# V and the large convolutions in 64x128 row tiles, as two halves with swapped PSUM banks, interleaved with K and R

## The chip, the cores and the metric

The kernel runs on one core of one Trainium2 chip. The core has a matrix engine (PE, TensorE), a vector engine (DVE), an activation engine (ACT), a general engine (POOL) and a sync engine (SP), each of which works through its own instructions in order, and 16 DMA engines that they share. Matmuls read SBUF and write PSUM, which has 128 partitions and 8 banks of 512 fp32 each. The metric is the time of one execution on the device, in microseconds (us); a lower one is better.

## The reference

x is 8 sequences of 4160 rows of 192 channels. A causal convolution of 7 taps comes first, with softmaxed weights shared by the 24 channels of each of 8 heads; then a channel mix:

```python
# attention stage: y[s, h, :] = sum over k of softmax(weight)[h, k] * x[s - 6 + k, h, :]
out = np.einsum('hk,bskhg->bshg', w, x_unf)
...
# channel mix on y
x_prev = np.concatenate([np.zeros((B, 1, D), dtype=np.float32), x[:, :-1, :]], axis=1)
xk = mu_k * x + (1.0 - mu_k) * x_prev
xr = mu_r * x + (1.0 - mu_r) * x_prev
k = np.maximum(xk @ w_k, 0.0)            # 192 -> 1024
v = k * k @ w_v                          # 1024 -> 192
r = 1.0 / (1.0 + np.exp(-(xr @ w_r)))    # 192 -> 192
return (r * v).astype(np.float32)
```

## The kernel before, in words

**Pairs, steps, bundles.** The 8 sequences are worked in 4 pairs. A pair is cut into steps of 512 rows (256 at both ends of the first pair), and the last 64 rows of all sequences make a step at the end. Channels lie on partitions: yT holds 64 channels of one sequence on partitions 0 to 63 and of the other on 64 to 127, three times for 192. So K and R contract 64 rows at a time, and a matmul of the first sequence stands on the upper half of PE's array (rows 0 to 63), one of the second on the lower half, each with its own PSUM bank: 64x128 row tiles. A step of 512 rows needs 8 slots of K (128 of the 1024 hidden channels for both sequences, six matmuls of 512 columns, L520); a bundle is four slots. There are 65 bundles. R (`r`, L594) and V (`v`, L606, `v_mm`, L577) are worked in quads of 256 rows of both sequences, one of each in a bundle. V contracts 128 hidden channels at a time on the whole array: 32 matmuls of 192 columns a quad.

**Convolution.** x is loaded by POOL's DMA queue, casting to bf16, in groups of 120-row blocks (`groups`, L86). A conv matmul multiplies a banded matrix `toe` (128x128 per head) with a block of x. Groups 0 to 2 (`conv_small`) and 3 (`conv_full`, L331) use the whole array with blocks of 120 rows that share 6 rows with the block before. Groups 4 and up (`conv_mm`, L309) hold each block as two halves of 58 rows and use 64x64 tiles, four at a time; `load_x_halves` (L118) loads them so. A unit is as many heads as fill a PSUM bank; ACT evicts a unit (`conv_out`, L385). Groups 0 to 3 are transposed on PE (`tr`). The others go to DRAM (`y_write`, L393, four DMAs on SP's queue) and come back transposed (`y_read`, L403, one transposing DMA on SP's queue).

**Elementwise work.** DVE makes d = y[s] - y[s-1] (`diff`, L473), xk and xr = mu * d + y[s-1] (`mix`, L496 and L500), k squared (L563) and the product r * v from PSUM (L618). ACT applies relu to K (L549) and the sigmoid to R (L602). The product leaves by two DMAs a quad on SP's queue (L626).

**Order.** The order on every engine is written out by hand (`manual_schedule`): tables say which bundle issues what, and the loop at L764 walks the bundles: four slots of K and their relus, R, V, mixes, three squares, the product, the conv units, the last square, then `late` with y writes and reads. A group's units stand in the bundles 10 to 7 before its step's first bundle; its write stands in the bundle of the last unit, its read two bundles later (one for group 4). All PSUM tiles come from one ring of four buffers of two banks (`ring`, L53), so a tile waits until the tile four places before is read.

Of the kernel before, what the change touches and what calls it, by code (L numbers as in the profile page):

```python
# [10 lines left out]
ALU = mybir.AluOpType  # L11
# [3 lines left out]
def kernel(  # L15
# [23 lines left out]
    HB = 58  # L39
# [46 lines left out]
    groups, base = [], []  # L86
    for p in range(NPAIR):
        blk0 = 0
        for nb, s, on_pe in (
            ((3, 0, True), (4, 1, True), (4, 2, True), (5, 3, True), (10, 4, False), (10, 6, False))  # L90
            if p == 0
            else ((10, 0, False), (10, 2, False), (10, 4, False), (6, 6, False))
        ):
            groups.append((p, blk0, nb, first_bundle[first_step[p] + s], on_pe))
            if on_pe:
                base.append(blk0 * BLK)
            elif groups[-2][4] or blk0 == 0:
                base.append(blk0 * BLK)
            else:
                base.append(base[-1] + 2 * HB * groups[-2][2])  # L100
            blk0 += nb
# [4 lines left out]
    def x_tile(g):  # L106
        p, blk0, nb, _, _ = groups[g]
        xb = three.tile([P, GB, 2, D], BF16, tag="xb", name="xb")
        xbs[g] = xb
        if g > 4:  # L110

            nc.vector.memset(xb[0:1, 0, 0, 0:2], 0.0)
        if blk0 == 0:
            nc.gpsimd.memset(xb[0:32, 0, :, :], 0.0)  # L114
        if g > 3 and base[g] + 2 * HB * nb >= S:
            nc.gpsimd.memset(xb[:, nb - 1, :, :], 0.0)

    def load_x_halves(g):  # L118
        p, _, nb, _, _ = groups[g]
        xb = xbs[g]  # L120
        for s in range(2):
            b = 2 * p + s
            for i in range(2):
                full = []
                for m in range(nb):
                    r0 = base[g] + (2 * m + i) * HB - HALO
                    lo, hi = max(0, -r0), min(Q, S - r0)
                    if lo == 0 and hi == Q:
                        full.append(m)
                    elif hi > lo:  # L130
                        nc.gpsimd.dma_start(  # L131
                            out=xb[i * Q + lo : i * Q + hi, m, s, :], in_=x[b, r0 + lo : r0 + hi, :]
                        )
                nc.gpsimd.dma_start(  # L134
                    out=xb[i * Q : (i + 1) * Q, full[0] : full[-1] + 1, s, :],
                    in_=bass.AP(
                        tensor=x.tensor,
                        offset=x.offset + (b * S + base[g] + (2 * full[0] + i) * HB - HALO) * D,
                        ap=[[D, Q], [2 * HB * D, len(full)], [1, D]],
                    ),  # L140
                )

    def load_x(g):
        p, blk0, nb, _, _ = groups[g]
        if g > 3:
            return load_x_halves(g)
        xb = xbs[g]
        for s in range(2):
# [5 lines left out]
            t0 = blk0 * BLK - HALO  # L154
            nc.gpsimd.dma_start(  # L155
# [144 lines left out]
    def pieces(c0, c1):  # L300
        cuts = [c0] + [a for a in range(Q, D, Q) if c0 < a < c1] + [c1]
        return list(zip(cuts, cuts[1:]))

    def conv_units(g):
        n = min(H, BANK // (G * groups[g][2]))
        return [range(h, min(H, h + n)) for h in range(0, H, n)]


    def conv_mm(g, c):  # L309
        nb = groups[g][2]  # L310
        if c == 0:
            ys[g] = two.tile([P, GB, 2 * D], BF16, tag="y", name="y")
        ps = ring.tile([P, 2, BANK], FP32, tag="k", name="ps_c")
        hs = conv_units(g)[c]
        w = G * len(hs)
        nn = nb // 2
        conv_ps[g, c] = ps
        for k, h in enumerate(hs):
            for j in range(2):
                for i in range(2):  # L320
                    nc.tensor.matmul(  # L321
                        out=ps[j * Q : (j + 1) * Q, i, 0 : nb * w].rearrange("p (n s c) -> p n s c", n=nn, s=2)[
                            :, :, :, k * G : (k + 1) * G
                        ],
                        lhsT=toe[i * Q : (i + 1) * Q, h, i * Q : (i + 1) * Q],
                        rhs=xbs[g][i * Q : (i + 1) * Q, j * nn : (j + 1) * nn, :, h * G : (h + 1) * G],
                        start=True,
                        stop=True,
                    )

    def conv_full(g, c, copy):  # L331
        nb = groups[g][2]
        if c == 0:
            ys[g] = two.tile([P, GB, 2 * D], BF16, tag="y", name="y")
        y = ys[g][:BLK, :nb, :].rearrange("p n (c s q) -> p n c s q", c=NC, s=2)
        ps2 = ring.tile([P, 2, BANK], FP32, tag="k", name="ps_c")
        w = 2 * G
        banks = [ps2[:, k, 0 : nb * 2 * w].rearrange("p (n s c) -> p n s c", n=nb, s=2) for k in range(2)]
        for k, ps in enumerate(banks):
            for i in range(2):  # L340
                h = 4 * c + 2 * k + i
                nc.tensor.matmul(
                    out=ps[:, :, :, i * G : (i + 1) * G],
                    lhsT=toe[:, h, :],
                    rhs=xbs[g][:, :nb, :, h * G : (h + 1) * G],
                    start=True,
                    stop=True,
                )
        for k, ps in enumerate(banks):
            c0 = (4 * c + 2 * k) * G  # L350
            for a, b in pieces(c0, c0 + w):
                copy(
                    out=y[:, :, a // Q, :, a % Q : a % Q + b - a], in_=ps[:BLK, :, :, a - c0 : b - c0]
                )
# [22 lines left out]
    def conv_out(g, c, copy):  # L377
        nb = groups[g][2]
        hs = conv_units(g)[c]
        ps = conv_ps.pop((g, c))  # L380
        c0, c1 = hs[0] * G, hs[-1] * G + G
        src = ps[:, :, 0 : nb * (c1 - c0)].rearrange("p i (n s c) -> p i n s c", n=nb // 2, s=2)
        y = ys[g][:, :nb, :].rearrange("p (n i) (c s q) -> p i n c s q", i=2, c=NC, s=2)
        for a, b in pieces(c0, c1):
            copy(out=y[:, :, :, a // Q, :, a % Q : a % Q + b - a], in_=src[:, :, :, :, a - c0 : b - c0])  # L385

    def new_yT(p):
        yTs[p] = two.tile([P, 3, -(-(YC + NBLK * BLK) // 16) * 16], BF16, tag="yT", name="yT")
        y_drams[p] = dram.tile([S + 2 * P, 2 * D], BF16, tag=f"y{p % 2}", name="y_dram")
# [3 lines left out]
    def y_write(g):  # L393
# [3 lines left out]
        for j in range(2):  # L397
            r0 = base[g] + j * nb * HB
            rows = y_drams[p][r0 : r0 + nb * HB, :].rearrange("(n t) c -> t n c", t=HB)
            for t0, t1 in ((0, HB // 16 * 16), (HB // 16 * 16, HB)):  # L400
                nc.sync.dma_start(out=rows[t0:t1], in_=ys[g][j * Q + t0 : j * Q + t1, :nb, :])

    def y_read(g):  # L403
        p, blk0, nb, _, _ = groups[g]
        r0 = base[g] // 16 * 16
        r1 = min((base[g] + 2 * nb * HB) // 16 * 16, S)
# [70 lines left out]
    def mix(s, i, sl=slice(0, NC)):  # L477
# [3 lines left out]
        if sl.start == 0:  # L481
            (xks, xrs)[i][s] = two.tile([P, NC, STEP], BF16, tag=("xk", "xr")[i], name=("xk", "xr")[i])
        t = (xks, xrs)[i][s]
        if s == 0 and i == 0:
            c = sl.start
# [9 lines left out]
        for c in range(sl.start, sl.stop):  # L495
            nc.vector.tensor_scalar(  # L496
                out=t[:, c, :L], in0=d[:, c, :L], scalar1=mu[:, i, c : c + 1], scalar2=None, op0=ALU.mult
            )
        o = shaped(s, t[:, sl, :L])
# [111 lines left out]

    def tile_of(s, j, k):
# [37 lines left out]
    early, first, rq, xt, mixes, vq, vo, late = ({} for _ in range(8))  # L650
# [4 lines left out]
    def conv(g, c):  # L655
        if g < 3:
            act_, dve_ = nc.scalar.copy, nc.vector.tensor_copy
            return conv_small(g, (act_, act_, dve_ if g == 0 else act_))
        if g == 3:
            return conv_full(g, c, nc.scalar.copy)  # L660
        conv_mm(g, c)
        conv_out(g, c, nc.scalar.copy)

    for g, (p, blk0, nb, fb, on_pe) in enumerate(groups):
        nx = len(conv_units(g))
# [8 lines left out]
        for i, b in enumerate(xs):  # L674
            at(xt, b, conv, g, i)
# [13 lines left out]
    for s, (p, t0, L, n0, ns) in enumerate(steps):  # L689
# [4 lines left out]
        at(mixes, fb - 1, diff, s)  # L694
        at(mixes, fb - 1, mix, s, 0)
        at(mixes, last_bundle[s] - (s < LAST), mix, s, 1)
        if s == LAST - 1 or s < LAST and steps[s + 1][0] > p:
            at(late, fb - 1, keep_tail, p)
    for s, j, vb in quads:
        if s == LAST:  # L700
            at(late, vb, v_last, s, j)
            at(rq, vb - 1, r, s, j)
        else:
            at(vq, vb, v, s, j)
            at(vo, vb, v_out, s, j)
            at(rq, vb - 1, r, s, j)
# [51 lines left out]

    with tc.manual_schedule():
        prologue()  # L760
        for b in range(-20, 0):
            for table in (early, first, rq, xt, mixes, vq, vo, late):
                assert b not in table, b
        for b in range(quads[-1][2] + 1):  # L764
            ns = bundles[b] if b < len(bundles) else ()
            run(early, b)
            for part in (ns[:2], ns[2:]) if b == 0 else (ns,):
                if part:
                    k_section(part)
                for n in part:  # L770
                    k_relu(n)
# [44 lines left out]
```

## Time and profile before

| what | value |
|---|---|
| median of three runs | 434.31 us (433.28 to 436.19) |
| the profiled execution | 434.77 us, span 433.1 us |
| PE | 418.1 us busy, 5045 matmuls |
| DVE | 378.4 us busy, 678 instructions |
| ACT | 348.2 us busy, 427 instructions |
| POOL | 62.4 us busy, 101 instructions |
| mean granted PE clock | 0.999 |
| DMA | 64.73 MB, mean 149 GB/s |

Busy times are a share of the span, from the first instruction to the last; what the execution has beside its span (1.7 us) is start and end. An engine's busy share says how full it is, not whether its work decides the end: that is read from the chain of work that ended last, followed back from the last instruction. In a row of groups, `L577 PE MATMUL ps_v<-wv,k 128*128 128x192 bf16` is line 577, an operation of PE that writes ps_v from wv and k, on 128 x 128 of the array, with 192 columns streamed. Matmuls overlap, so a row's mean duration (246 ns for V) is longer than the distance between two starts. SPq is SP's instruction queue, whose DMA issues are not counted as busy.

### The profile page before, as it was taken

What the parts mean: (1) busy time and instruction counts of PE and PEld (TensorE: products, weight loads), DVE (VectorE), ACT (ScalarE), POOL (GpSimd) and SP (SyncE); (2) the same over time, 40 slices, a digit from 0 to 9 for tenths busy, and PEclk for the clock granted to TensorE, in tenths of its full rate; (3) what the DMA queues carried; (4) which work ended last, traced back from release to release, by engine and by line L of the source; (5) the groups of instructions that cost most, each with busy time, mean ns of one, the idle gap of its engine ahead of it and who ended that gap; (6) DMA issues with size and microseconds to landing.
All of it is one profiled execution on the core that took longest, in us unless ns stands there. A gap on an engine that the chain in (4) does not pass through costs nothing.

```text
span 433.1 us, 12070 instructions
## 1 busy us (share of the span) xinstructions
PE 418.1 (97%) x5045; PEld 293.4 (68%) x5045; DVE 378.4 (87%) x678; ACT 348.2 (80%) x427; POOL 62.4 (14%) x101
## 2 busy tenths in 40 slices
PE   7779999989999999999999999999999999999995
PEld 3456667757867766776677667766766776667785
DVE  5879888798988899888889989888898889999983
ACT  5787988978988888888889878988898888777780
POOL 7651002203310200303030200203000000000000
PEclk9999999999999999999999999999999999999999
DMA  7998885999896976689896994496845484321223
GB/s 127 192 160 126 201 175 107 183 232 184 176 184 180 175 196 124 89 197 156 195 183 160 181 208 108 97 222 126 192 116 136 118 205 87 111 66 47 74 75 109
DMA packets 136444, 64.73 MB, mean 149 GB/s; under 512 B 87122, under 2 KB 136006, under 8 KB 136390
## 3 DMA queue, kind: packets, MB, share of 16 engines
q1 hardware_dynamic: 96536, 48.29, 47.2%
q0 software_dynamic: 38960, 15.08, 30.2%
q8 instruction: 39, 0.64, 0.6%
q10 hardware_dynamic: 894, 0.61, 0.5%
q14 instruction: 15, 0.12, 0.1%
HBM read 30.75 MB, written 36.96 MB: 156 GB/s over the span
## 4 chain that ended last, share of the span: by engine, by line
PE 85%; DMA 5%; DVE 4%; ACT 3%; issue 2%; POOL 1%; SPq 0%; ACTq 0%
PE ps_v L577 39%; PE ps_k L520 35%; PE ps_r L594 7%; PE ps_c L321 3%; DMA yT<-y_dram 3%; ACT k_sb L549 2%; DMA wk<-in_moe_w_k_dram 2%; DVE k L563 1%; DVE xk L496 1%; PE ps_t L420 1%; ACT y L385 0%; DVE d L473 0%; DVE o_sb L618 0%; POOL xb L155 0%; DVE yT L429 0%
## 5 line engine op out<-in xcount | busy, mean ns | idle before, releaser
L549 ACT ACTIVATE k_sb<-ps_k 128x1024 bf16<-128x1024 f32 x260 | 246.4, 1047 | 23.3 <-PE ps_k L520 23.0
L520 PE MATMUL ps_k<-xk,wk 64*128 64x512 bf16 (+1 forms) x1632 | 181.0, 367 | 3.5 <-ACT k_sb L549 1.2
L577 PE MATMUL ps_v<-wv,k 128*128 128x192 bf16 x2080 | 182.7, 246 | 1.3 <-ACT k_sb L549 1.3
L577 PEld LDWEIGHTS <-k 128*128 128x128 bf16 x2080 | 168.7, 98 | 11.3 <-issue 11.3
L563 DVE TENSOR_TENSOR k<-k_sb 128x1024 bf16<-128x1024 bf16 x260 | 167.3, 685 | 0.4 <-ACT k_sb L549 0.4
L520 PEld LDWEIGHTS <-wk 64*128 64x128 bf16 x1632 | 74.9, 94 | 89.3 <-issue 11.3
L618 DVE TENSOR_TENSOR o_sb<-ps_v,r_sb 128x768 f32<-128x768 f32 x64 | 61.3, 957 | 35.2 <-PE ps_v L577 31.3
L385 ACT CAST y<-ps_c 128x960 bf16<-128x960 f32 (+7 forms) x81 | 50.8, 669 | 45.8 <-PE ps_c L321 45.8
L134 POOL DMA_DIRECT2D xb<-in_x_dram x56 | 40.3, 731 | 205.3 <-PE ps_k L520 157.2
L602 ACT ACTIVATE r_sb<-ps_r 128x768 bf16<-128x768 f32 x65 | 56.1, 863 | 1.3 <-PE ps_r L594 1.3
L594 PEld LDWEIGHTS <-xr 64*128 64x128 bf16 x780 | 34.0, 94 | 17.7 <-issue 2.5
L594 PE MATMUL ps_r<-wr,xr 64*128 64x192 bf16 x780 | 42.9, 243 | 2.0 <-ACT k_sb L549 1.1
L473 DVE TENSOR_TENSOR d<-yT 128x1536 bf16<-128x1536 bf16 (+2 forms) x35 | 31.1, 889 | 1.9 <-DMA yT<-y_dram 1.8
L496 DVE TENSOR_SCALAR xk<-d,mu 128x512 bf16<-128x512 bf16 (+1 forms) x99 | 31.2, 371 | 1.2
L500 DVE TENSOR_TENSOR xr<-xr,yT 128x1536 bf16<-128x1536 bf16 (+1 forms) x33 | 31.0, 938 | 1.1
L500 DVE TENSOR_TENSOR xk<-xk,yT 128x1536 bf16<-128x1536 bf16 (+1 forms) x32 | 30.4, 950 | 1.1
L496 DVE TENSOR_SCALAR xr<-d,mu 128x512 bf16<-128x512 bf16 (+1 forms) x102 | 29.4, 345 | 0.0
L321 PE MATMUL ps_c<-xb,toe 64*64 64x240 bf16 (+1 forms) x448 | 20.0, 265 | 0.0
L321 PEld LDWEIGHTS <-toe 64*64 64x64 bf16 x448 | 8.3, 105 | 7.7 <-issue 7.7
L457 POOL COPY y_tail<-yT 128x195 bf16<-128x195 bf16 x4 | 1.5, 364 | 69.7 <-DMA yT<-y_dram 69.7
L131 POOL DMA_DIRECT2D xb<-in_x_dram x14 | 7.6, 545 | 1.4 <-POOL xb L114 0.9
L714 PE MATMUL warm<-zeros,ones_t 128*128 128x512 bf16 x16 | 5.5, 521 | 1.8 <-DVE zeros L729 1.8
(55 smaller groups left out, 55.5 us busy)
## 6 DMA issues: line engine op xcount, KB each, us to landing
out_dram<-o_sb SPq DMA_DIRECT2D x128, 192.0 KB
xb<-in_x_dram POOLq DMA_DIRECT2D x36, 240.0 KB, 7.0
y_dram<-y SPq DMA_DIRECT2D x22, 360.0 KB
xb<-in_x_dram POOLq DMA_DIRECT2D x10, 216.0 KB, 5.4
y_dram<-y SPq DMA_DIRECT2D x22, 75.0 KB
y_dram<-y SPq DMA_DIRECT2D x6, 216.0 KB
xb<-in_x_dram POOLq DMA_DIRECT2D x6, 144.0 KB, 6.3
xb<-in_x_dram POOLq DMA_DIRECT2D x4, 192.0 KB, 7.8
```

Of the source, the lines that this page charges most:

```text
L134: nc.gpsimd.dma_start(out=xb[i * Q : (i + 1) * Q, full[0] : full[-1] + 1, s, :], in_=bass.AP(tensor=x.tensor, offset=x.offset + (b * S + b ...
L321: nc.tensor.matmul(out=ps[j * Q : (j + 1) * Q, i, 0 : nb * w].rearrange("p (n s c) -> p n s c", n=nn, s=2)[:, :, :, k * G : (k + 1) * G], ...
L385: copy(out=y[:, :, :, a // Q, :, a % Q : a % Q + b - a], in_=src[:, :, :, :, a - c0 : b - c0])
L496: nc.vector.tensor_scalar(out=t[:, c, :L], in0=d[:, c, :L], scalar1=mu[:, i, c : c + 1], scalar2=None, op0=ALU.mult)
L500: nc.vector.tensor_tensor(out=o, in0=o, in1=y_of(s, sl, 0), op=ALU.add)
L520: nc.tensor.matmul(out=ps[:, i, f * L : (f + 1) * L], lhsT=wk[r, c, fs], rhs=xk[r, c, :L], start=c == 0 and f == 0, stop=c == NC - 1 and f ...
L549: nc.scalar.activation(out=k_sb, in_=ps.rearrange("p a b -> p (a b)"), func=AF.Relu)
L563: nc.vector.tensor_tensor(out=o, in0=i, in1=i, op=ALU.mult)
L577: nc.tensor.matmul(out=o, lhsT=k2s[s][:, f, t * P : (t + 1) * P], rhs=wv[:, f, :], start=(f == 0), stop=(f == NF - 1),)
L594: nc.tensor.matmul(out=ps[:, i, k * D : (k + 1) * D], lhsT=xr[q, c, ts], rhs=wr[q, c, :], start=c == 0, stop=c == NC - 1,)
L602: nc.scalar.activation(out=r_sbs[s, j], in_=ps[:, :, 0 : 2 * D], func=AF.Sigmoid)
L618: nc.vector.tensor_tensor(out=o_sb.rearrange("p (b t) d -> p b (t d)", b=2), in0=v_ps.pop((s, j)), in1=r_sbs.pop((s, j)), op=ALU.mult,)
```

## The change

- V: each 128-row contraction becomes two of 64 rows, on the two row tiles, and is done in two halves. In half 0 the upper row tile adds into bank 0 for the first sequence's rows while the lower adds into bank 1 for the second's; in half 1 the banks are swapped, and each bank gets the part that is missing.
- Convolution of groups 3 and up: the same, with one head (two for groups of five blocks) in each bank, on 120-row blocks; a pair of heads is chosen so that both banks are evicted by one instruction. The halves of 58 rows, `load_x_halves` and `base` go. The groups of the first pair are 3, 4, 4, 5, 10 and 9 blocks, of the others 10, 10, 10 and 5, the last one bound to the eighth step in place of the seventh. A group's y write is one DMA of 120 partitions.
- Between the halves `clobber_nop` puts an instruction on SP's queue. In the built program it waits for the last matmul of half 0, and the first matmul of half 1 waits for it. Bundles 1 to 64 hold one for each conv unit and one for each V quad, 111 in all.
- A bundle is written out as K slot, half of conv, K slot, other half, R, half of V, (half of conv), K slot, (other half), other half of V, K slot. Relus and squares follow their slots; the squares of slots 2 and 3 move to the next bundle; DVE's differences, scales and adds are spread over two bundles, and the product stands at the bundle's end.
- On SP the order within a bundle is: the SP instructions of the conv and V halves, the two output DMAs, then a y write or a y read.

```diff
-            ((3, 0, True), (4, 1, True), (4, 2, True), (5, 3, True), (10, 4, False), (10, 6, False))
+            ((3, 0, True), (4, 1, True), (4, 2, True), (5, 3, True), (10, 4, False), (9, 6, False))
             if p == 0
-            else ((10, 0, False), (10, 2, False), (10, 4, False), (6, 6, False))
+            else ((10, 0, False), (10, 2, False), (10, 4, False), (5, 7, False))
...
     def conv_units(g):
-        n = min(H, BANK // (G * groups[g][2]))
-        return [range(h, min(H, h + n)) for h in range(0, H, n)]
+        if groups[g][2] * 4 * G <= BANK:
+            return [((0, 1), (6, 7)), ((2, 3), (4, 5))]
+        return [((0,), (1,)), ((3,), (4,)), ((6,), (7,)), ((2,), (5,))]
+
+    def conv_mm(g, c, half):
...
+        for k in range(last + 1):
             for i in range(2):
+                q = slice(i * Q, (i + 1) * Q)
+                bank = (i + half) % 2
+                h = unit[bank][k]
                 nc.tensor.matmul(
+                    out=banks[:, bank, :, :, k * G : (k + 1) * G],
+                    lhsT=toe[q, h, :],
+                    rhs=xbs[g][q, :nb, :, h * G : (h + 1) * G],
+                    start=half == 0 and k == 0,
+                    stop=half == 1 and k == last,
                 )
+        if half == 0:
+            nc.sync.clobber_nop([nc.sync.lower_ap(conv_ps[g, c])])
...
-        for j in range(2):
-            r0 = base[g] + j * nb * HB
-            rows = y_drams[p][r0 : r0 + nb * HB, :].rearrange("(n t) c -> t n c", t=HB)
-            for t0, t1 in ((0, HB // 16 * 16), (HB // 16 * 16, HB)):
-                nc.sync.dma_start(out=rows[t0:t1], in_=ys[g][j * Q + t0 : j * Q + t1, :nb, :])
+        nc.sync.dma_start(
+            out=y_drams[p][blk0 * BLK : (blk0 + nb) * BLK, :].rearrange("(n t) c -> t n c", t=BLK),
+            in_=ys[g][:BLK, :nb, :],
+        )
...
+    def v_rows(s, j, half):
+
+        if half == 0:
+            v_ps[s, j] = ring.tile([P, 2, BANK], FP32, tag="k", name="ps_v")[:, :, 0 : 2 * D]
+        for k in range(2):
+            for f in range(NF):
+                for i in range(2):
+                    q = slice(i * Q, (i + 1) * Q)
+                    bank = (i + half) % 2
+                    t = tile_of(s, j, 2 * bank + k)
+                    nc.tensor.matmul(
+                        out=v_ps[s, j][:, bank, k * D : (k + 1) * D],
+                        lhsT=k2s[s][q, f, t * P : (t + 1) * P],
+                        rhs=wv[q, f, :],
+                        start=half == 0 and k == 0 and f == 0,
+                        stop=half == 1 and k == 1 and f == NF - 1,
+                    )
+        if half == 0:
+            nc.sync.clobber_nop([nc.sync.lower_ap(v_ps[s, j])])
...
+            if s == 4:
+                at(mix_a, fb - 1, diff, s)
+            else:
+                at(mix_c, fb - 2, diff, s)
+            at(mix_a, fb - 1, scale, s, 0, 0)
+            at(mix_b, fb - 1, scale, s, 0, 1, 2)
+            at(mix_b, fb - 1, scale, s, 1, 0)
+            at(mix_c, fb - 1, add_y, s, 0)
+            at(mix_a, fb, scale, s, 1, 1)
+            at(mix_b, fb, scale, s, 1, 2)
+            at(mix_b, fb, add_y, s, 1)
...
+    def conv_half(unit, half):
+        if unit is not None:
+            conv_mm(*unit, half)
+            if half == 1:
+                conv_out(*unit, nc.scalar.copy)
...
+    def bundle_rest(b, ns):
+
+        units = xt.get(b, []) + [None, None]
+        quad = vq.get(b, [None])[0]
+        for n in bundles[b - 1][2:] if b > 1 else ():
+            k_square(n)
+        run(mix_a, b)
+        k_mm(ns[0])
+        k_relu(ns[0])
+        k_square(ns[0])
+        run(mix_b, b)
+        conv_half(units[0], 0)
+        k_mm(ns[1])
+        conv_half(units[0], 1)
+        k_relu(ns[1])
+        k_square(ns[1])
+        run(rq, b)
+        run(first, b)
+        if quad:
+            v_rows(*quad, 0)
+        conv_half(units[1], 0)
+        k_mm(ns[2])
+        conv_half(units[1], 1)
+        k_relu(ns[2])
+        if quad:
+            v_rows(*quad, 1)
+        run(mix_c, b)
+        k_mm(ns[3])
+        k_relu(ns[3])
+        if quad:
+            v_out(*quad)
+        run(late, b)
```

## The prediction

> **What bounds the kernel now.** I read the page first, then the chain of waits, then one bundle of the steady part on PE and on SP's queue. PE is busy nearly all the time and carries the chain:
>
> ```profile
> PE 418.1 (97%) x5045; PEld 293.4 (68%) x5045; DVE 378.4 (87%) x678; ACT 348.2 (80%) x427; POOL 62.4 (14%) x101
> PE 85%; DMA 5%; DVE 4%; ACT 3%; issue 2%; POOL 1%; SPq 0%; ACTq 0%
> ```
>
> SP has no part in the chain. What its two kinds of y transfers take on its queue stands in the answers for their source lines (ns: least/median/most, then first and last start):
>
> ```profile
> L407 SPq DMA_TRANSPOSE yT<-y_dram x14: 2065/4382/6837, 50.5 to 365.2; - x14
> L401 SPq DMA_DIRECT2D y_dram<-y x56: 321/487/2337, 43.7 to 354.8; - x56
> ```
>
> SP spends 2 to 7 us on each transpose read, and today nobody waits for that. Now the two timelines, PE and then SP's queue (start, duration):
>
> ```profile
> 194.73 0.40 PE L321 MATMUL ps_c<-xb,toe 64*64 64x240 bf16 x8
> 195.06 2.76 PE L520 MATMUL ps_k<-xk,wk 64*128 64x512 bf16 x24
> 197.66 0.66 PE L594 MATMUL ps_r<-wr,xr 64*128 64x192 bf16 x12
> 198.25 2.81 PE L577 MATMUL ps_v<-wv,k 128*128 128x192 bf16 x32
> 201.00 0.40 PE L321 MATMUL ps_c<-xb,toe 64*64 64x240 bf16 x8
> ```
> ```profile
> 195.82 0.89 SPq L626 DMA_DIRECT2D out_dram<-o_sb  x2
> 196.88 4.71 SPq L407 DMA_TRANSPOSE yT<-y_dram  x1
> 202.09 0.89 SPq L626 DMA_DIRECT2D out_dram<-o_sb  x2
> ```
>
> A bundle with a conv unit takes 6.27 us (194.73 to 201.00), one without 5.94 us. PE has no hole in it; what it loses is at the change of shape. Start to start, V matmuls stand 82.5 ns apart, but V to conv takes 176 ns, R to V 175, conv to K 195 against 104 for a conv round, V to K 178; K to R, both 64x128, takes the usual 213. So a change of shape costs 0.09 us, three times a bundle with conv, twice without.
>
> **The change, part by part.** All sums are against the profiled execution, 434.77 us (span 433.1), 0.46 above the median of 434.31.
>
> *V in row tiles.* 2080 full matmuls become 4160 of 64x192. R (L594) is that very shape: its pairs start 82.5 ns apart, 3 ns within a pair. 2080 pairs x 82.5 ns is what V takes now: difference 0. The doubled instruction count could cost: V asks for an instruction (matmul or weight load) each 20.6 ns through 64 of them; R shows this for 24 in a row, and K's 256-wide steps sustain 106 ns a pair, 26.5 ns each. If that were the limit, V would lose 24 ns a pair, 2080 x 24 = 50 us; I take 0, since R has the shape, and keep 50 as the far end.
>
> *Changes of shape go.* 63 R to V (0.093), 49 V to conv (0.093), 49 conv to K (0.091) and 13 V to K (0.095): -5.9 -4.6 -4.5 -1.2 = -16.2 us.
>
> *Conv in row tiles.* Now 448 matmuls run four at a time; the spacings inside the units come to 7.5 us, the last rounds (40 x 0.104, 9 x 0.064) to 4.7, together 12.3 us. After it there are 50 units (eleven groups of nine or ten blocks with four, three of five blocks with two). Each half streams 480 columns on both row tiles at once; L342's 240 columns stand 102 ns apart, so a unit takes 4 x 0.102 = 0.41 us, together 20.3: +8.0. Group 3 (eight matmuls of 240 before, eight pairs of 240 after) stays level. Net on PE: **-8 us**: bundles of 6.10 and 5.70 us.
>
> *Loads and y.* POOL issues two to four x loads a group in place of four to eight (0.73 us each, POOL busy 14%): 0, the loads stand bundles ahead of their conv. The differences move up to the end of the second bundle before their K, the read is issued in the fifth: 11 us after it leaves SP, 0.
>
> *ACT and DVE.* Per conv bundle ACT does four relus (3.80), a sigmoid (0.86) and an eviction (0.96): 5.62 in 6.10, covered. DVE's two kinds of bundle are four squares (0.61 each), one product (0.88), and either two scales, a mix add and a difference (0.60 + 0.88 + 0.88), or four scales and an add (1.20 + 0.88): 5.7 and 5.4, under 6.10 and, on average, under 5.70. I cost the reordering at 0; without that cover it is about 0.2 us in 17 bundles, 3 us. Reading PSUM buffers round the ring of four, the next K's second slot waits for V's product; the product is out 1.2 us after V, PE comes there at 1.28 to 1.48.
>
> *The new wait.* Each half 0 ends with an instruction on SP that waits for PE, and half 1 (a PE matmul) waits for SP. The queue is in order: the program puts, in each bundle, conv's and V's SP instruction, then the two output DMAs (which wait for DVE's product), then the y write or the transpose read. So the next bundle's conv half 1 waits for everything that the bundle before left on SP, and behind that matmul stand R, V and all that follows on PE. PE comes to conv half 1 this long after V ends: k3 0.64 + k0 0.64 + conv half 0.20 + k1 0.64 = 2.12 us. SP is free, from the same row of today's trace (V's slots end 0.09 before conv starts):
> - Plain bundles: output DMAs end 2.07 us after V in most. Two event instructions on SP (17 to 28 ns, 50 apart) and PE's wake are about 0.2 (an estimate from SP's spacing): PE waits 0.17, with the longer issues in the tail 0.2. 24 conv bundles: **+5 us**, ends 0 and 10. It eats the gain there: 6.10 + 0.17 is 6.27 again.
> - After a transpose read: it starts 2.25 after V. The eleven reads of about 1,150 rows took 3.58, 5.36, 4.05, 6.33, 6.84, 4.71, 5.71, 5.55, 5.46, 3.88, 3.84, mean 5.03, ending 7.3 us after V; the next SP instruction stands 0.05 behind in most, so SP is held. PE waits 7.3 + 0.2 - 2.1 = 5.4 us, eleven times: 59. Of the three short ones (2.73, 2.07, 3.31) two precede a conv unit, 2.7 each, and one only V half 1, which PE reaches 4.38 after V: 1.4. **+66 us**; with all at the shortest 48, near the longest 85.
> - After a y write: four issues today, from 2.17 after V, 3.39 us for ten blocks. One issue of 1200 rows of 768 bytes takes their place, and no row shows it: at least the shortest single issue, 0.45, at most all four, 3.4. The third issue of a group takes 1.6 us against 0.44 for an equal first one, so the queue fills; I take 2.8, nearer the four as the bytes are the same. Eight large ones before conv cost 2.17 + 2.8 + 0.2 - 2.1 = 3.0, two small ones 1.4, three before V alone 0.8: **+29 us**, ends 5 and 42.
>
> *PE going cold.* The warm-ups at the start (L714) stood 427 ns apart nine times, then 216: a cold start loses 9 x 0.21 = 1.9 us. A hole of 1.2 us in today's trace (before 18.78) cost nothing. The new holes of 5 us lie between; ends 0 and 11 x 1.9 = 21: I take **+10 us**, half, as nothing separates them.
>
> The Trainium skill ("TensorE: Matmul & The Clock Gate", Part 1) says that an idle window of about 3.4 us, free-running, halves PE's clock. An estimate from that page: a hole of 5.4 us covers such a window in 2.0/3.4 = 58% of cases; 11 x 0.58 x 1.9 = 12, the sum 539 in place of 537. Today's steady part has no hole long enough to say.
>
> Sum: 434.8 - 8 + 5 + 66 + 29 + 10 = **537 us**, 24% slower. The waits do not overlap each other, since each is in a bundle of its own, and nothing is left to catch up afterwards: PE then goes at its own rate again.
>
> **Rivals.**
> 1. *Milder holes.* The y write costs its shortest, PE stays warm, SP's wait in plain bundles is 0: 434.8 - 8 + 66 + 5 = 498, and 480 with the shortest reads. For it: SP's longer issues vary by two for equal sizes, so they hang on other traffic, which the holes thin out. Against: the reads come to 63 us on SP (14 of a mean of 4.53) whatever stood beside them.
> 2. *SP lets the event instruction pass* while the read is still being issued, the case on the other side. Its place is the SP queue at 196.88 to 201.59, its price is all SP waits, 434.8 - 8 = 427, 2% faster. It decides when SP runs the event within 2.0 us of V's end. Against it: after the six longest reads the output DMAs start 1.4 to 3.0 us after V today, in place of 1.2.
> 3. *The same, with DVE the bound.* SP passes, but DVE's row (378 us busy) in its new order misses the product by 0.2 us in 50 bundles: 427 + 10 = 437, no difference.
> 4. *PE's instruction stream* limits V: 537 + 50 = 587, or 548 on top of the mild case.
>
> **How the numbers follow.** Forecast 537: 55%. Mild holes 498: 28%. Instruction stream: 8%. SP passes, 427: 6%. DVE, 437: 3%. What can be told from no change is about 1%, so faster is 6%, the same 2% (a third of rival 3 falls outside), slower 92%. The range takes the first two cases with their ends: below, 434.8 - 8 + 48 + 5 = 480; above, the forecast with long reads (+19), long writes (+13), a cold start at each (+11) and longer plain waits (+5) gives 585.
>
> **What would show it.** PE waits at the second conv half for SP, in 13 bundles after the reads at 3 to 7 us and in 10 after the writes; the transpose rows still 2 to 7 us long; V pairs at 82.5 ns; no 0.09 us between K, V and conv; a clock below 1.0 in the slices with holes; DVE and ACT at a lower share. I am wrong if the PE waits on SP stay under 0.3 us, if the write's single issue is near 0.5 us, or if V's pairs stand wider than 90 ns.

## The result and the profile after

| | before | after |
|---|---|---|
| median, range | 434.4 us (433.28 to 436.19) | 532.17 us (531.19 to 534.84) |
| ratio of the times | | 1.2256, 95% interval 1.2191 to 1.232 |
| the profiled execution, its span | 434.77, 433.1 us | 534.84, 533.1 us |
| mean granted PE clock | 0.999 | 0.923 |

The change makes the kernel 22.6% slower; the forecast was 537 us, 24%. The page of the kernel after shows PE no longer full, and its clock below full speed in many slices of the span. The lines are the busy times, the clock in 40 slices, the chain of work that ended last, and one group of instructions (count, busy us, mean ns, idle us just before it and what ended most of that):

```profile
PE 439.1 (82%) x6845; PEld 332.8 (62%) x6845; DVE 384.2 (72%) x678; ACT 351.1 (66%) x407; POOL 48.9 (9%) x73
...
PEclk9999796997979969998797998999789898999999
...
PE 26%; SPq 4%; DVE 1%; POOL 0%; issue 0%; DVEq 0%
...
L291 PE MATMUL ps_c<-xb,toe 64*128 64x480 bf16 (+2 forms) x240 | 41.9, 358 | 81.4 <-SPq L299 81.3
```

L291 is the conv matmul, and L299 is the `clobber_nop` on SP between its halves. 81 of the 94 us that PE was idle (533.1 - 439.1) stand before conv matmuls and end with SP. No other engine has become the bound: DVE went from 87% to 72%, ACT from 80% to 66%. The chain follows only part of the span here (its shares add up to 31%), so the waits are read from the timelines.

The transpose reads and the y writes on SP's queue, by source line (ns: least/median/most, then first and last start):

```profile
L367 SPq DMA_TRANSPOSE yT<-y_dram x14: 1474/4720/10222, 52.2 to 472.2; - x14
L359 SPq DMA_DIRECT2D y_dram<-y x14: 353/450/529, 45.0 to 460.7; - x14
```

Reads now take up to 10.2 us; a write takes 0.45 us in one issue. The timeline of PE, then of SP's queue, round one read (start, duration, what, and in brackets the idle time before and what ended it):

```profile
244.25 0.38 PE L291 MATMUL ps_c<-xb,toe 64*128 64x480 bf16 x2
244.46 0.83 PE L490 MATMUL ps_k<-xk,wk 64*128 64x512 bf16 x6
254.97 0.59 PE L291 MATMUL ps_c<-xb,toe 64*128 64x480 bf16 x2 [9.68 <-SPq L299]
255.32 1.19 PE L564 MATMUL ps_r<-wr,xr 64*128 64x192 bf16 x12
256.28 2.79 PE L592 MATMUL ps_v<-wv,k 64*128 64x192 bf16 x32
...
263.61 0.38 PE L291 MATMUL ps_c<-xb,toe 64*128 64x480 bf16 x2
263.81 0.67 PE L564 MATMUL ps_r<-wr,xr 64*128 64x192 bf16 x12
264.30 1.50 PE L592 MATMUL ps_v<-wv,k 64*128 64x192 bf16 x32
```
```profile
244.16 0.89 SPq L616 DMA_DIRECT2D out_dram<-o_sb  x2
245.16 9.63 SPq L367 DMA_TRANSPOSE yT<-y_dram  x1
```

Half 0 of the conv unit runs at 244.25. SP has begun a read before its instruction for the unit comes up in the queue; the read ends at 254.79, and conv half 1 starts at 254.97, 0.18 us later. Behind it R takes 1.19 us and half of V 2.79, against 0.67 and 1.50 in the next bundle: PE runs at half speed for a while after the hole. The clock shows that too. These are windows of the kernel after (start:end, us, busy us of PE, PE's weight loads, DVE, ACT and POOL with their counts, granted clock, DMA share, GB/s), the first in the hole at 413.5, the second behind it:

```profile
413.40:416.80 3.40, 0.09 (x2) 0.00 (x0) 2.52 (x5) 0.57 (x1) 0.00 (x0) 1.00 0.96 224
416.90:420.30 3.40, 2.96 (x36) 2.73 (x37) 0.42 (x1) 2.33 (x3) 0.00 (x0) 0.50 0.66 149
```

### The profile page after: what moved, and what is told of

The parts are those of the page before. It is cut to its first block, busy times and chain, and to the rows that moved or that the text cites. A ratio compares the mean times of both kernels' runs of the same rounds, so it can differ in the third digit from the quotient of the medians.

```text
span 533.1 us, 15786 instructions
## 1 busy us (share of the span) xinstructions
PE 439.1 (82%) x6845; PEld 332.8 (62%) x6845; DVE 384.2 (72%) x678; ACT 351.1 (66%) x407; POOL 48.9 (9%) x73
## 5 line engine op out<-in xcount | busy, mean ns | idle before, releaser
L519 ACT ACTIVATE k_sb<-ps_k 128x1024 bf16<-128x1024 f32 x260 | 259.1, 1031 | 77.2 <-PE ps_k L490 77.0
L533 DVE TENSOR_TENSOR k<-k_sb 128x1024 bf16<-128x1024 bf16 x260 | 177.8, 688 | 95.1 <-ACT k_sb L519 87.3
L490 PE MATMUL ps_k<-xk,wk 64*128 64x512 bf16 (+1 forms) x1632 | 205.7, 374 | 1.9 <-DVE xk L470 1.0
L592 PE MATMUL ps_v<-wv,k 64*128 64x192 bf16 x4032 | 201.9, 252 | 0.6 <-ACT k_sb L519 0.6
L592 PEld LDWEIGHTS <-k 64*128 64x128 bf16 x4032 | 185.1, 98 | 14.4 <-issue 2.8
L490 PEld LDWEIGHTS <-wk 64*128 64x128 bf16 x1632 | 88.6, 96 | 55.7 <-issue 3.8
L336 ACT CAST y<-ps_c 120x960 bf16<-120x960 f32 (+4 forms) x67 | 50.7, 782 | 89.8 <-PE ps_c L291 89.8
L291 PE MATMUL ps_c<-xb,toe 64*128 64x480 bf16 (+2 forms) x240 | 41.9, 358 | 81.4 <-SPq L299 81.3
L291 PEld LDWEIGHTS <-toe 64*128 64x128 bf16 x240 | 16.3, 96 | 105.5 <-issue 94.6
L125 POOL DMA_DIRECT2D xb<-in_x_dram x34 | 30.8, 912 | 281.7 <-PE ps_c L291 161.3
L564 PEld LDWEIGHTS <-xr 64*128 64x128 bf16 x780 | 39.7, 101 | 10.2 <-DVE xb L105 2.0
```

What stands on the lines that cost most here:

```text
L291: nc.tensor.matmul(out=banks[:, bank, :, :, k * G : (k + 1) * G], lhsT=toe[q, h, :], rhs=xbs[g][q, :nb, :, h * G : (h + 1) * G], start=hal ...
L336: copy(out=bass.AP(tensor=y.tensor, offset=y.offset + d0, ap=[y.ap[0], [d1 - d0, 2], [2 * D, nb], [Q, 2], [1, n]],), in_=bass.AP(tensor=ps ...
L490: nc.tensor.matmul(out=ps[:, i, f * L : (f + 1) * L], lhsT=wk[r, c, fs], rhs=xk[r, c, :L], start=c == 0 and f == 0, stop=c == NC - 1 and f ...
L519: nc.scalar.activation(out=k_sb, in_=ps.rearrange("p a b -> p (a b)"), func=AF.Relu)
L533: nc.vector.tensor_tensor(out=o, in0=i, in1=i, op=ALU.mult)
L564: nc.tensor.matmul(out=ps[:, i, k * D : (k + 1) * D], lhsT=xr[q, c, ts], rhs=wr[q, c, :], start=c == 0, stop=c == NC - 1,)
```

## The experiments

Two readings could explain the result. In the first, SP's queue is the cause: its reads and writes hold the instruction that conv half 1 waits for. In the second, the new form itself costs the time: halves with a wait between them, row tiles, or the traffic to DRAM. Forecasts are quoted as they were recorded ahead of each run.

### The wait moved to PE's own queue

The instruction between the halves goes to PE, directly before half 1, for conv and V alike. Matmuls, order, loads and y transfers stay. (The trace of the kernel after holds 52 conv units and 63 V quads in two halves, so 115 such instructions, where the section on the change says 111.)

```diff
+        if half == 1:
+            nc.tensor.clobber_nop([nc.tensor.lower_ap(conv_ps[g, c])])
...
-        if half == 0:
-            nc.sync.clobber_nop([nc.sync.lower_ap(conv_ps[g, c])])
...
+        else:
+            nc.tensor.clobber_nop([nc.tensor.lower_ap(v_ps[s, j])])
...
-        if half == 0:
-            nc.sync.clobber_nop([nc.sync.lower_ap(v_ps[s, j])])
```

> The changed kernel, with the instruction between the halves on PE's own queue, directly before half 1, in place of SP's; K stands between, so half 0 is long done there. Nothing else is moved. Theory A (SP's queue: PE waits for an SP instruction that stands behind output DMAs, y writes and transposing reads, and its clock halves in the long holes): all holes go and the clock stays at 1.0; bundles of 5.7 and 6.1 us; 434.8 - 8 = 427 us, between 422 and 432. Theory B (the row tiles of V, the written-out order or DVE's new order cost the time themselves): over 500 us.

Measured: 431.75 us (430.7 to 432.67) beside 433.6 for the kernel before; ratio 0.9951, 0.9933 to 0.9969. The 100 us are gone, and with them every PE wait on SP. A bundle in the timeline of PE now has no bracket, and from conv half 0 to the next bundle's it takes 309.29 - 303.16 = 6.13 us:

```profile
303.16 0.38 PE L293 MATMUL ps_c<-xb,toe 64*128 64x480 bf16 x2
303.36 0.83 PE L490 MATMUL ps_k<-xk,wk 64*128 64x512 bf16 x6
304.01 0.38 PE L293 MATMUL ps_c<-xb,toe 64*128 64x480 bf16 x2
304.21 0.67 PE L564 MATMUL ps_r<-wr,xr 64*128 64x192 bf16 x12
304.71 1.50 PE L594 MATMUL ps_v<-wv,k 64*128 64x192 bf16 x32
306.03 0.83 PE L490 MATMUL ps_k<-xk,wk 64*128 64x512 bf16 x6
306.68 1.50 PE L594 MATMUL ps_v<-wv,k 64*128 64x192 bf16 x32
...
309.29 0.38 PE L293 MATMUL ps_c<-xb,toe 64*128 64x480 bf16 x2
```

So the queue is the cause, and the form is not. Some 5 us to the expected 427 are missing; one bundle at 80 us, 6.8 us longer than the others, holds them, and a later part takes that up.

### Only conv's wait, or only V's, moved to PE

One of the two edits above each. After V of the bundle before, PE comes to the second half of conv after 2.1 us and, in a bundle with conv, to that of V after 4.8 (308.00 to 312.81 us in the kernel with both waits on PE; the prediction's 4.38 is for a bundle without conv). With conv's wait on PE and V's on SP:

```diff
+        if half == 1:
+            nc.tensor.clobber_nop([nc.tensor.lower_ap(conv_ps[g, c])])
-        if half == 0:
-            nc.sync.clobber_nop([nc.sync.lower_ap(conv_ps[g, c])])
```

> The changed kernel with only the conv units' instruction on PE; V's stays on SP. Theory A: after a read SP is free T + 2.25 + 0.2 us after V, T the read's length; PE comes to V half 1 about 4.8 us after V, so a hole is T - 2.3: with the thirteen lengths of the changed kernel's profile 43 us in all, five of them over 3.4 us and cold (10): 427 + 43 + 10 = 480 us, between 455 and 500; no hole after y writes or in plain bundles. Theory B: as the changed kernel, 532.

With V's wait on PE and conv's on SP:

```diff
+        else:
+            nc.tensor.clobber_nop([nc.tensor.lower_ap(v_ps[s, j])])
...
-        if half == 0:
-            nc.sync.clobber_nop([nc.sync.lower_ap(v_ps[s, j])])
```

> The changed kernel with only V's instruction on PE; the conv units' stays on SP. Theory A: conv half 1 comes first after a read and takes the whole hole, V's SP instruction was covered behind it: no gain, 525 to 535 us, the same holes of 4 to 10 us at L291's second half. Theory B with V's wait as the cause: near 430.

Measured, one run of each: 484.35 us with conv's wait on PE, 534.92 with V's. The second is the changed kernel's time. In the first the hole moves to the second half of V, which needs SP as well, and is shorter by what PE can still do before it. PE, then SP's queue:

```profile
222.59 0.83 PE L490 MATMUL ps_k<-xk,wk 64*128 64x512 bf16 x6
230.74 2.74 PE L592 MATMUL ps_v<-wv,k 64*128 64x192 bf16 x32 [7.32 <-SPq L600]
```
```profile
220.63 9.98 SPq L367 DMA_TRANSPOSE yT<-y_dram  x1
```

A read of 9.98 us costs PE 7.32 here, and one of 9.63 cost it 9.68 above. The waits of PE by what ended them (us in total, times, longest), in the kernel with conv's wait on PE and then in that with V's:

```profile
PE ps_v L592 <- SPq L600: 45.1, 11, 7.3
```
```profile
PE ps_c L291 <- SPq L299: 82.7, 26, 11.4
```

Whichever wait PE meets first after the read takes the hole; freeing the later one alone frees nothing. Where only V waits for SP, all eleven waits follow one of the eleven long reads, and none follows a y write: the write is over long before.

### V on the whole array again

From the kernel with both waits on PE: V's matmuls get their 128x128 form back, two of the four tiles in each of the two places, without a wait. The conv part stays.

```diff
-            for f in range(NF):
-                for i in range(2):
...
+            v_mm(v_ps[s, j][:, half, k * D : (k + 1) * D], s, tile_of(s, j, 2 * half + k))
```

> As e1 (no wait on SP), but V on the whole array again, 32 matmuls of 128x128, two of its four row tiles of output in each half, so that only V's shape differs. If a change of shape costs 0.09 us: four a bundle (R to V, V to K, K to V, V to K) x 62 = 23 us over e1, 450 us, between 445 and 456; V's matmuls 82.5 ns apart in both. If the row form of V itself costs (doubled instructions), it is faster than e1.

Measured: 453.2 us (453.12 to 453.31); ratio 1.0446, 1.0427 to 1.0465. That is 21.5 us over the kernel with row tiles. The timeline of PE shows where:

```profile
303.62 0.66 PE L564 MATMUL ps_r<-wr,xr 64*128 64x192 bf16 x12
304.21 1.49 PE L547 MATMUL ps_v<-wv,k 128*128 128x192 bf16 x16
305.64 0.82 PE L490 MATMUL ps_k<-xk,wk 64*128 64x512 bf16 x6
306.39 1.49 PE L547 MATMUL ps_v<-wv,k 128*128 128x192 bf16 x16
307.82 1.47 PE L490 MATMUL ps_k<-xk,wk 64*128 64x512 bf16 x12
```

R lasts as long as with V in row tiles, but V starts 0.59 us after R's start in place of 0.50; from the first half of V to K it is 1.43 us in place of 1.32, and from those six matmuls of K to V 0.75 in place of 0.65. Four changes of shape of 0.09 to 0.11 us make 0.42 us a bundle: bundles with conv take 6.56 us in place of 6.14, those without 6.15 in place of 5.73. Over 63 bundles that is 26.5 us; the times differ by 5 us less because the kernel with row tiles has other waits that are shorter here or missing, in the bundle at 80 us above all and in a hole of 1.6 us at 207.7 us. V's own matmuls stand 82.5 to 83 ns apart in both forms. So the row form of V costs nothing by itself, and what it saves is the change of shape.

### V in row tiles without a cover

From the kernel before: V alone in row tiles, the two halves back to back, with the wait on PE between them.

```diff
 def v(s, j):
+        for half in range(2):
+            if half == 1:
+                nc.tensor.clobber_nop([nc.tensor.lower_ap(v_ps[s, j])])
+            for k in range(2):
+                ...  # the row-tile matmuls of the change
```

> The kernel before with one part of the change alone: V in row tiles, two halves with swapped banks, back to back, the second half behind an instruction on PE that waits for the first; conv, order, loads and DMAs as before. Theory A (a wait between halves must be covered): R to V loses its change of shape, 63 x 0.093 = -5.9 us; the wait stands open, a matmul's 246 ns less its 82 ns slot plus a wake of about 0.1 us (estimate), 0.25 x 64 = +16: 434 + 10 = 444 us, between 438 and 450. If the wait costs nothing, 428.

Measured: 445.47 us (445.17 to 446.84); ratio 1.0274, 1.0249 to 1.0299. The timeline of PE:

```profile
202.01 0.66 PE L594 MATMUL ps_r<-wr,xr 64*128 64x192 bf16 x12
202.51 3.09 PE L617 MATMUL ps_v<-wv,k 64*128 64x192 bf16 x64
205.53 0.40 PE L321 MATMUL ps_c<-xb,toe 64*64 64x240 bf16 x8
```

R to V costs no change of shape any more, but V takes 205.53 - 202.51 = 3.02 us against 2.75 in the kernel before (198.25 to 201.00): the open wait between the halves costs about 0.28 us, more than the change of shape that it saves. In each of the 64 quads one distance between two starts, 0.35 us in place of 0.08, stands at the middle of V, between the halves. In the changed kernel a K slot stands there, and the same wait on PE costs nothing that can be seen (6.14 us a bundle against 6.10 forecast without any wait).

### The changed kernel without most loads of x

Groups 6 and up are filled with zeros by POOL in place of being loaded. This leaves out those loads, and the convolution of those groups computes on zeros; the rest of the work and the waits on SP stay.

```diff
+        if g > 5:
+            nc.gpsimd.memset(xb[:, :nb, :, :], 0.0)
+            return
```

> The changed kernel without the x loads of the pairs 2 to 4 (groups 6 and up are filled with zeros on POOL), so this leaves out part of the input traffic; all else, SP's instructions between the halves too, stays. If the reads are long because x loads run beside them: all reads of 1200 rows take 3.8 to 4.0 us as those without loads do now, the holes are about 4.0 us in place of 4 to 10, 28 us less and some 5 less at half clock: 500 us, between 488 and 512. If the length is the reads' own: 532.

Measured, one run: 514.62 us, 2.6 above the top of the expected range. The reads, by source line, and two rows of the waits:

```profile
L370 SPq DMA_TRANSPOSE yT<-y_dram x14: 1483/3701/4064, 52.2 to 452.3; - x14
```
```profile
PE ps_c L294 <- SPq L302: 53.7, 26, 4.2
...
PE ps_k L493 <- DVE xk L473: 7.2, 6, 1.9
```

Every read of some 1,200 rows now takes 3.5 to 4.1 us, where the changed kernel has 3.8 to 10.2, and PE's waits on SP fall from 81.3 to 53.7 us, by the 28 us that were expected. So loads of x in flight lengthen a read, and a read without them still holds the queue for 3.5 us and more. The saving as a whole is smaller than expected, because K now waits for DVE's xk, which takes 7.2 us of PE's time (1.0 in the changed kernel), and because eleven stretches at half clock are still there. K's waits come with the fills, as the timelines of POOL and DVE show:

```profile
134.55 3.30 POOL L115 MEMSET xb<- 128x3840 bf16 x1
```
```profile
135.41 2.65 DVE L467 TENSOR_SCALAR xk<-d,mu 128x512 bf16<-128x512 bf16 x1
```

In each of the nine fills of ten blocks a scale of DVE that otherwise takes 0.35 us takes 2.2 to 2.8 us, and ends 0.1 to 0.2 us after the fill.

### The group's load moved: two tries

The kernel with both waits on PE had one bundle of 12.93 us, at 80 us. In its timelines POOL, SP, PE and DVE meet there:

```profile
69.26 1.88 POOL L125 DMA_DIRECT2D xb<-in_x_dram  x2 [38.39 <-PE ps_c L293]
```
```profile
69.71 8.38 SPq L367 DMA_TRANSPOSE yT<-y_dram  x1
```
```profile
84.05 0.38 PE L293 MATMUL ps_c<-xb,toe 64*128 64x480 bf16 x2 [2.77 <-DMA xb<-in_x_dram]
86.68 1.47 PE L490 MATMUL ps_k<-xk,wk 64*128 64x512 bf16 x6 [2.26 <-DVE xb L105]
```
```profile
84.80 0.96 DVE L433 TENSOR_TENSOR d<-yT 128x1536 bf16<-128x1536 bf16 x1 [5.74 <-DMA yT<-y_dram]
```

POOL issues the load of group 7 in bundle 8, 0.45 us before SP starts a read. Both come late: conv waits for x, DVE for yT, and K behind DVE. The first try issues the load in bundle 5.

```diff
-            b = {4: 1, 5: 1, 6: 2, 7: 8, 8: 10, 9: 13}.get(g)
+            b = {4: 1, 5: 1, 6: 2, 7: 5, 8: 10, 9: 13}.get(g)
```

> e1 with the x load of group 7 in bundle 5 in place of 8. In e1 one bundle of 12.9 us (at 80 to 93 us) holds PE waits for that load and DVE waits for the read that ran beside it, 6.8 us over the others, with 3.4 us of half clock. If the load beside the read is the cause, the bundle falls to 6.1 us: 431.75 - 6.8 = 425 us, between 423 and 428. If the read alone is late, no change: 431.

Measured: 434.23 us (432.47 to 437.43); ratio 1.0008, 0.9987 to 1.003. The expectation missed. The bundle at 80 us is fine, but the load now meets the read before. SP's queue and the waits of DVE:

```profile
50.41 11.77 SPq L367 DMA_TRANSPOSE yT<-y_dram  x1
```
```profile
DVE d L433 <- DMA yT<-y_dram: 9.0, 1, 9.0
```

That read took 4.42 us in the kernel it was made from; here K waits 8.95 us at 70 for what DVE makes of it. The second try issues the load in bundle 6, between the two reads.

```diff
-            b = {4: 1, 5: 1, 6: 2, 7: 8, 8: 10, 9: 13}.get(g)
+            b = {4: 1, 5: 1, 6: 2, 7: 6, 8: 10, 9: 13}.get(g)
```

> e1 with the x load of group 7 in bundle 6, between the reads of groups 4 (bundle 4) and 5 (bundle 7), where bundle 8 (e1) and bundle 5 (e7) each met a read: a load of 480 KB takes about 9 us to land, the gap between the reads is 54 to 70 us. If the meeting of load and read makes the hole (6.8 us in e1, 9.1 in e7), both reads are 3.5 to 4.5 us long, no bundle after the first four is over 6.6 us, and the time is 431.75 - 6.8 = 425 us, between 423 and 427. If one of the two is late in any order: 430 or more.

Measured: 424.5 us (423.43 to 424.74) beside 433.33 for the kernel before; ratio 0.9787, 0.977 to 0.9804, about 2% faster than the kernel before. SP's queue, and the page's busy times and chain:

```profile
50.18 3.93 SPq L367 DMA_TRANSPOSE yT<-y_dram  x1
...
69.73 3.26 SPq L367 DMA_TRANSPOSE yT<-y_dram  x1
```
```profile
PE 409.0 (97%) x6845; PEld 315.7 (75%) x6845; DVE 381.8 (90%) x678; ACT 347.6 (82%) x407; POOL 48.8 (12%) x73
...
PE 86%; DMA 6%; DVE 3%; ACT 1%; POOL 1%; issue 0%; SPq 0%; DVEq 0%
```

Both reads are short, PE is at 97% with the chain on it, and SP has dropped out of the chain. Later reads of this kernel still take up to 11.29 us; PE does not wait for them.

## Why the prediction was right

The sign, the place and the mechanism stand: PE waits for an instruction on SP's queue that stands behind a transpose read, and moving that instruction alone takes 100 us away. But the sum of 537 met the measured 534.8 (the profiled execution) because three terms were off in different directions: that it met the time to within 0.5% is luck.

| term | forecast | measured | from |
|---|---|---|---|
| PE's own work, shapes and conv | -8 | -10 | 424.56 in the last experiment's profiled execution (group 7's load two bundles earlier, too), against 434.77 |
| plain bundles, wait for SP | +5 | +2.6 | 24 x (6.25 - 6.14) |
| holes after reads | +66 | +75.7 | 13 holes in the trace |
| holes after writes | +29 | +8.3 | 10 holes in the trace |
| PE at half clock | +10 | +22.5 | eleven bundles, below |

From 424.56, which has the change without SP's waits, the four measured waits add up to 424.56 + 2.6 + 75.7 + 8.3 + 22.5 = 533.7, beside 534.84. A stretch at half clock that stands outside this sum, at 24 us, follows no wait on SP but one of 1.7 us on DVE; the two bundles round it take some 1.2 us more than with both waits on PE, about what the sum lacks.

**PE's own work: right.** Conv bundles without a hole take 6.25 us after (forecast 6.10 + 0.17), 6.14 with the wait on PE; those without conv 5.72 (forecast 5.70). No 0.09 us is left between K, V and conv. V's pairs stand 82 ns apart, so its doubled instruction count cost nothing; the two matmuls of a pair start 19 to 20 ns apart, as R's do in this kernel (3 ns in the kernel before).

**Cover on DVE and ACT: right.** Both have less share of a longer span, and where PE is not held (the last experiment) DVE has 90% and no bundle waits for the product.

**Holes after reads: right in place, size low by 10.** A hole is taken here as the distance from the K slot to conv half 1, less the 0.65 us of the slot. The eleven large ones came to 72.3 us (4.0 to 10.44) against the forecast 59, the two short ones before conv to 3.4 against 5.4; the one that was to stand at V cost nothing. The forecast took today's read lengths, a mean of 5.03 us. The change itself made them 6.28. The packets of POOL's queue that start while a read is issued point to the loads: in the kernel before the large reads have 0 to 1,176 beside them, 4,800 in all, and in the kernel after 0 to 2,592, 9,000 in all. Without loads they are at 3.5 to 4.1 us, as the experiment shows. The term should have allowed for a read of the new kernel standing differently to the loads; its far end of 85 did.

**Holes after writes: the step that failed.** The forecast took 2.8 us for the single issue, "nearer the four as the bytes are the same". The row is 0.35 to 0.53 us: its lower end, 0.45, was right, and the sentence that said "I am wrong if the write's single issue is near 0.5 us" came true. Eight holes are 0.62 to 0.72 us; two are 1.31 and 1.67, because the output DMAs ahead of the write took longer (one of 1.25 us, and a pair of 1.58 in place of 0.89). The four issues before (two of 360 KB and two of 75) took 3.39 us on the same queue, the one of 900 KB now 0.45. What makes the four slow was not tried and stays open.

**PE at half clock: low by half.** The forecast took half of eleven cold starts of 1.9 us. In the trace the granted clock is 0.5 in a stretch after each of the eleven holes of 4.0 us and more, and after none of SP's holes of 1.7 and less. The periods of these eleven bundles sum to 162.9 us; less 68.1 for their normal length and 72.3 for the holes leaves 22.5, 2.0 each on average. So the row from the kernel's start gave a price close to that average, and the count was wrong, eleven in place of five or six. The estimate from the Trainium skill ("TensorE: Matmul & The Clock Gate", Part 1) that a hole of 5.4 us covers an idle window in 58% of cases gave 12 us. Its free-running window is seen: the half-clock stretches last 3.4 to 10.2 us, in multiples of 3.413, and start on a grid of 3.413 us. But the window needn't be idle as a whole. Here are three windows on the grid round a hole of 4.0 us (columns as above):

```profile
440.88:444.29 3.41, 1.92 (x20) 0.98 (x17) 3.24 (x6) 1.94 (x2) 0.00 (x0) 1.00 0.42 121
444.29:447.70 3.41, 1.06 (x25) 1.06 (x26) 0.96 (x1) 0.64 (x1) 0.00 (x0) 0.99 1.16 251
447.70:451.11 3.41, 3.41 (x38) 2.68 (x34) 1.57 (x2) 1.94 (x3) 0.00 (x0) 0.51 0.09 19
```

PE was busy for 1.06 of 3.41 us in the middle one, 69% idle, and ran at half clock in the next.

**The rivals.** SP does not pass: its event instruction waits for the end of the read, 0.18 us ahead of PE's start. DVE is not the bound, and PE's instruction stream sustains V's pairs at 82 ns. The milder case was right about the write and wrong about the clock; with the measured writes in it the forecast's sum would have been 537 - 21 = 516, and the two terms that were too low hid that.

## What to carry to other kernels

An instruction that only orders two pieces of work of one engine belongs on that engine's queue, with other work between the pieces: on a queue that also issues DMAs it stands behind whatever is ahead of it there, and each of the eleven holes of 4 us and more cost 2 us more, on average, through the clock. Where PE runs one shape all through, the wait between the halves is free under a slot of K, and 0.28 us a quad without it. Before a load is moved, look which other transfer will be on its way at the new time: three places for one load made 431.75, 434.23 and 424.5 us.

## What the runs showed of the hardware

- The issue of one transposing read of a large group (some 1,200 rows) holds SP for 3.2 to 4.7 us with at most 46 packets of POOL's queue beside it, over the kernel before, the kernel after and the runs with both waits on PE, and for 5.0 to 11.8 with 260 and more. The count alone does not set it: some 1,060 packets went with 8.67 and with 11.32 us, 1,182 with 5.27; and with V on the whole array again one read took 5.38 us with none, one 5.23 with 33.
- A hole of 3.59 us, with conv's wait on PE, was not followed by half clock: the two windows on the grid that it touches were 53% and 48% idle. Every wait on SP from 3.69 us (in the run without loads) up was, and the last window ahead of those stretches was 61% to 100% idle. But the idle share of one window doesn't set it alone: the stretches at 24.4 us in the kernel after and at 23.1 us with conv's wait on PE follow windows that were 50% idle, and the window from 314.5 us of the kernel after, 54% idle, was followed by one at full clock. What separates these stays open.
- In the kernel with both waits on PE one hole of 1.6 us at 207.7 us is put down to nothing that the profile shows; it was not followed up.
